# Two decode attentions in one kernel: wq as nine rows per partition, both sides' q from one set of matmuls

## The chip, the cores and the metric

The kernel runs on one core of one Trainium2 chip. The metric is the device time of one execution in microseconds. The core has five engines with an instruction stream each: TensorE (PE, with its weight loads listed apart as PEld), VectorE (DVE), ScalarE (ACT), GpSimd (POOL) and SyncE (SP). 16 DMA engines move data between HBM and the on-chip memory of 128 partitions (SBUF). TensorE writes into PSUM, eight banks of 128 x 512 float32.

## The reference

Two independent decode steps, A and B, each for one token; their outputs are put side by side. Everything is bfloat16.

```python
Hq, Dh = 32, 128          # 16 kv heads, Sk = 8192, x is [1, 1, 576]
q = (x @ wq).reshape(B, Sq, Hq, Dh).transpose(0, 2, 1, 3)      # wq is [576, 4096]
k = jnp.repeat(k_cache[:, :, Sk - W:, :], rep, axis=1)         # A: the last W = 2048 keys; B: all 8192
v = jnp.repeat(v_cache[:, :, Sk - W:, :], rep, axis=1)
p = softmax(einsum("bhqd,bhkd->bhqk", q, k) * (Dh ** -0.5))
o = einsum("bhqk,bhkd->bhqd", p, v)
out = o.transpose(0, 2, 1, 3).reshape(B, Sq, Hq * Dh) @ wo     # wo is [4096, 576]
```

All inputs together are 102.76 MB: the two wq and the two wo have 4.72 MB each, A's keys and values 8.39 MB each, B's 33.55 MB each.

## The kernel before

**How it is written.** The kernel is a list of operations for each engine (`Prog`, L37). An operation names the operations and loads that it waits for, and `emit` (L59) turns the names into semaphore waits. The order on an engine is the order in which the operations were written down; an engine that waits holds up everything behind it on that engine.

**The loads.** All big loads are issued by SP, in one order, onto one DMA queue. They go into a ring in SBUF of 144 KB per partition (`ring`, `RING` L31). `place` (L167) gives each load the next stretch of the ring; where the stretch was used before, SP waits ahead of the issue for the last users of what lay there. Each load has one of 24 semaphores in turn; from the 25th load on SP also waits for the users of the load 24 places earlier. The order is: wq of A (two loads), wq of B (two loads), K of A's first four heads (K0), K1, V0, K2, V1, K3, V2, the K of B's first four heads in two halves (K4.0, K4.1), V3, K5 in two halves, V4, K6, V5, K7, V6, V7 in two halves, then wo of A in one load and wo of B in five. (A unit is four kv heads: units 0 to 3 are A's, 4 to 7 are B's.) The first eight loads have free room in the ring. V1 and K3 take the place of the main load of A's wq, V2 that of A's last rows and of the start of B's wq, K4.0 that of the rest of B's wq and of K0.

**wq.** wq of a side has 576 rows of 8 KB. The main load brings the first 512 rows: partition p holds rows 4p to 4p + 3, 32 KB (L191). The second load, "tail", brings the last 64 rows as 128 half rows of 4 KB: partition p holds half p mod 2 of row 512 + p // 2 (L193). A's and B's wq lie one after the other in the ring and both use all 128 partitions.

**x.** ACT's queue loads the two x into one partition (`xrow`). For each side (L266), DVE copies the last 64 elements of x twice each (`xd`, L267); five matmuls of depth 1 against a row of ones put x on the partitions and repeat it over 128 columns (`xT`, L276); DVE casts the four main columns to bf16 (`xr`, L279), and multiplies the fifth by `par`, 1 on even or on odd partitions, for the left and the right half rows (L282).

**The q matmuls.** For each side and each of eight column blocks of 512 (L299 to L313), five matmuls of depth 128 add up a block of q in one of four PSUM banks; since x is repeated over the columns of the stationary operand, all 128 output rows are the same q. 80 matmuls in all; the first 40 need only A's wq, the last 40 only B's. ACT copies each block into `qsb` (`qe`, L314), DVE turns two blocks at a time in 32 x 32 squares into `ktb` (`qT`, L317), and after a side's last turn four DVE copies put the pieces into the stationary operands of the score matmuls, `za` for A (`z0`, L329) and `zb` for B (`z1`, L324).

**The rest.** Then unit after unit: DVE turns K slabs of 2048 elements per partition out of the ring into `ktb` (`turn`, L350; the first one waits for all eight `z` copies, since `ktb` held q), PE makes scores (`score`, L367), DVE and PE find the maximum, ACT takes the exponential (L406), DVE turns the probabilities (L414, L418), and PE multiplies with V out of the ring (`pv`, L431). At the end PE multiplies the outputs with wo (`F`, L510), first A's, then B's as its five loads land, and two output transfers follow (L523).

Of the kernel before, what the change touches and what calls it, by code (L numbers as in the profile page):

```python
# [14 lines left out]
DM = 576  # L15
# [4 lines left out]
SLAB = 2048  # L20
NQ = G // 4
# [4 lines left out]
W0 = 2 * (NB - 1)  # L26
ZW = 128 + W0
ZA = 128 + 24
BIG = 1e30
N0 = 320  # L30
RING = 72 * 1024  # L31
NSEM = 24
NKT = 3
NWO = [[32], [17, 8, 4, 2, 1]]


class Prog:  # L37
# [60 lines left out]
def bass_concat_heads__sliding_block_cached__gqa_block_cached__decode_kernel(nc, A_x, A_k_cache, A_v_cache, A_wq, A_wo,  # L98
                         B_x, B_k_cache, B_v_cache, B_wq, B_wo, out):
    xs, ks, vs = [A_x, B_x], [A_k_cache, B_k_cache], [A_v_cache, B_v_cache]  # L100
    wqs, wos = [A_wq, B_wq], [A_wo, B_wo]
# [4 lines left out]
    ring = nc.alloc_sbuf_tensor("ring", [128, RING], BF16)  # L106
    ktb = nc.alloc_sbuf_tensor("ktb", [128, NKT * SLAB], BF16)
# [3 lines left out]
    onesf = nc.alloc_sbuf_tensor("onesf", [128, 128], F32)  # L111
    onesb = nc.alloc_sbuf_tensor("onesb", [1, 128], BF16)
    xrow = nc.alloc_sbuf_tensor("xrow", [1, 2 * DM], BF16)
    xdup = nc.alloc_sbuf_tensor("xdup", [1, 2, 128], BF16)
    xrep = nc.alloc_sbuf_tensor("xrep", [128, 2, 6, 128], BF16)
    qsb = nc.alloc_sbuf_tensor("qsb", [128, 4, 512], BF16)

    zb = nc.alloc_sbuf_tensor("zb", [128, NQ, 4, ZW], BF16)

    za = nc.alloc_sbuf_tensor("za", [128, NQ, 4, ZA], BF16)  # L120
# [17 lines left out]
    par = nc.alloc_sbuf_tensor("par", [128, 2], F32)  # L138
# [9 lines left out]
    sb = [nc.alloc_psum_tensor("sb%d" % b, [128, 512], F32) for b in range(2)]  # L148
    qb = [nc.alloc_psum_tensor("qb%d" % b, [128, 512], F32) for b in range(2)]
    vb = [nc.alloc_psum_tensor("vb%d" % b, [128, 512], F32) for b in range(2)]  # L150
    mb = nc.alloc_psum_tensor("mb", [128, 512], F32)
    ob = nc.alloc_psum_tensor("ob", [128, 512], F32)

    def view(t, free, offset, dims, parts=128, p0=0):
        return bass.AP(tensor=t, offset=p0 * free + offset, ap=[[free, parts], *dims])

    pg = Prog(nc)
    op, load = pg.op, pg.load
    s_x = [nc.alloc_semaphore("s_x%d" % i) for i in range(2)]
    s_ld = [nc.alloc_semaphore("s_ld%d" % i) for i in range(NSEM)]  # L160
    s_out = nc.alloc_semaphore("s_out")
    s_row = [nc.alloc_semaphore("s_row%d" % i) for i in range(2)]

# [3 lines left out]
    def place(size, uses, issue, name):  # L167
        if at[0] + size > RING:
            at[0] = 0
        lo, hi = at[0], at[0] + size  # L170
        at[0] = hi
        deps = []
        for r in list(live):
            if r[0] < hi and lo < r[1]:
                deps += r[2]
                live.remove(r)
        n = nload[0]
        nload[0] += 1
        if n >= NSEM:
            deps += uses_of[n - NSEM]  # L180
        uses_of.append(list(uses))
        live.append((lo, hi, list(uses)))
        t = ring[:, lo:hi]
        load("sp", lambda e: issue(e, t), s_ld[n % NSEM], 16 * (n // NSEM + 1), deps=deps, name=name)
        return t

    wq_at = {}
    w = HQ * DH
    for P in range(2):
        uses = ["qmm%d.7" % P]  # L190
        main = wqs[P][0:512, :].rearrange("(p k) n -> p (k n)", k=4)  # L191
        wq_at[P, 0] = place(4 * w, uses, lambda e, t, main=main: e.dma_start(t, main), "wq%d.0" % P)
        tail = wqs[P][512:DM, :].rearrange("r (c n) -> (r c) n", c=2)  # L193
        wq_at[P, 1] = place(w // 2, uses, lambda e, t, tail=tail: e.dma_start(t, tail), "wq%d.1" % P)


    kv_at = {}
# [35 lines left out]
    def slab(kind, i, s):  # L233
# [10 lines left out]
       deps=["id0"], name="ident")  # L244
# [6 lines left out]
    for P in range(2):  # L251
        x = xs[P]
# [7 lines left out]
    for c in range(2):  # L260
        op("dve", lambda e, c=c: e.tensor_reduce(par[:, c:c + 1], view(identf, 128, c, [[2, 64]]), AX.X, ALU.add),
           deps=["identf"], name="par%d" % c)


    banks = [sb[0], sb[1], qb[0], qb[1]]
    for P in range(2):  # L266
        op("dve", lambda e, P=P: e.tensor_copy(  # L267
            view(xdup, 256, 128 * P, [[2, 64], [1, 2]], parts=1),
            view(xrow, 2 * DM, P * DM + 512, [[1, 64], [0, 2]], parts=1)), deps=["x%d" % P], name="xd%d" % P)
        for k in range(5):  # L270
            def mm(e, P=P, k=k):
                if k < 4:
                    lhsT = view(xrow, 2 * DM, P * DM + k, [[4, 128]], parts=1)
                else:
                    lhsT = xdup[0:1, P, :]
                return e.matmul(banks[2 * P + k // 4][:, (k % 4) * 128:(k % 4 + 1) * 128], lhsT=lhsT,  # L276
                                rhs=onesb[0:1, :], start=True, stop=True)
            op("pe", mm, deps=["x%d" % P, "onesb", "xd%d" % P], name="xT%d.%d" % (P, k))
        op("dve", lambda e, P=P: e.tensor_copy(  # L279
            xrep[:, P, 0:4, :].rearrange("p k m -> p (k m)"), banks[2 * P][:, :]), deps=["xT%d.3" % P], name="xr%d.0" % P)  # L280
        for c in range(2):
            op("dve", lambda e, P=P, c=c: e.tensor_scalar(  # L282
                xrep[:, P, 4 + c, :], banks[2 * P + 1][:, 0:128], par[:, c:c + 1], None, ALU.mult),
                deps=["xT%d.4" % P, "par%d" % c], name="xr%d.%d" % (P, 1 + c))

    op("dve", lambda e: e.tensor_reduce(clsb[:].rearrange("p (b r) -> p b r", r=2),
                                        view(identf, 128, 0, [[32, 4], [1, 2], [2, 16]]), AX.X, ALU.add),
       deps=["identf"], name="clsb")
    op("dve", lambda e: e.tensor_reduce(clsa[:], view(identf, 128, 0, [[1, 8], [8, 16]]), AX.X, ALU.add),
       deps=["identf"], name="clsa")  # L290
# [2 lines left out]
    op("dve", lambda e: e.tensor_scalar(mkl[:], view(ident, 128, 0, [[0, 16], [1, 4], [0, 2]], 4), -1.0, BIG,  # L293
                                        ALU.add, ALU.mult), deps=["ident"], name="mkl")

    XR = ["xr%d.%d" % (P, c) for P in range(2) for c in range(3)]

    KT = NKT * SLAB
    for P in range(2):  # L299
        for n in range(8):  # L300
            u = 8 * P + n
            bank = banks[u % 4]

            def mm(e, P=P, n=n, bank=bank):
                for k in range(5):
                    if k < 4:
                        lhsT, o = xrep[:, P, k, :], wq_at[P, 0][:, k * w + n * 512:k * w + (n + 1) * 512]
                    else:
                        lhsT, o = xrep[:, P, 4 + n // 4, :], wq_at[P, 1][:, (n % 4) * 512:(n % 4 + 1) * 512]
                    ins = e.matmul(bank[:, :], lhsT=lhsT, rhs=o, start=(k == 0), stop=(k == 4))  # L310
                return ins
            op("pe", mm, deps=["wq%d.0" % P, "wq%d.1" % P] + XR + (["qe%d" % (u - 4)] if u >= 4 else []),
               name="qmm%d.%d" % (P, n))  # L313
            op("act", lambda e, u=u, bank=bank: e.activation(qsb[:, u % 4, :], bank[:, :], ACT.Copy),  # L314
               deps=["qmm%d.%d" % (P, n)] + (["qT%d" % (u // 2 - 2)] if u >= 4 else []), name="qe%d" % u)
            if n % 2:
                op("dve", lambda e, u=u, n=n: e.transpose(  # L317
                    ktb[:, (n - 1) * 512:(n + 1) * 512].bitcast(I32),
                    qsb[:, u % 4 - 1:u % 4 + 1, :].rearrange("p a n -> p (a n)").bitcast(I32)),
                    deps=["qe%d" % (u - 1), "qe%d" % u] + (["z0.%d" % i for i in range(4)] if P else []),  # L320
                    name="qT%d" % (u // 2))
        for b in range(4):
            if P == 1:
                op("dve", lambda e, b=b: e.tensor_copy(  # L324
                    view(zb, NQ * 4 * ZW, 32 * b + W0, [[4 * ZW, NQ], [2 * ZW, 2], [ZW, 2], [1, 2]], 32, 32 * b),
                    view(ktb, KT, b * 256, [[1024, NQ], [64, 2], [1, 2], [128, 2]], 32, 32 * b)),
                    deps=["qT%d" % u for u in range(4, 8)] + ["zb0"], name="z1.%d" % b)
            else:
                op("dve", lambda e, b=b: e.tensor_copy(  # L329
                    view(za, NQ * 4 * ZA, ZA - 128 + 32 * b, [[4 * ZA, NQ], [2 * ZA, 2], [ZA, 2], [1, 8]], 32, 32 * b),  # L330
                    view(ktb, KT, 0, [[1024, NQ], [64, 2], [1, 2], [128, 8]], 32, 32 * b)),
                    deps=["qT%d" % u for u in range(4)] + ["za0"], name="z0.%d" % b)
    Z = ["%s.%d" % (z, b) for z in ("z0", "z1") for b in range(4)]
    QE = ["qe%d" % u for u in range(16)]


    k0 = [sum(nslab[:i]) for i in range(NU)]
# [218 lines left out]
```

## Time and profile before

| | before |
|---|---|
| three runs | 246.38, 246.15, 246.25 us (median 246.25) |
| span of the profiled execution | 245.2 us; its own run time is not given apart |
| DMA queue 1 (all big loads) | 4468 packets, 102.76 MB, 97.9% of 16 engines' span |
| PE, DVE, ACT, POOL busy | 172.3, 129.1, 24.3, 8.2 us |
| TensorE clock granted, mean | 0.82 of full speed |
| q matmuls (L310) | first at 14.60 us, last ends at 34.6 us |
| first K turn (L350) | 36.86 us |
| wo of A landed, PE starts on it | 232.3 us |

Stages are read from the windows: busy time of each engine between two moments, then the granted clock, the DMA engines' busy share and GB/s. A packet is counted into a window by its start, so a share can exceed 1. The trace also keeps every DMA packet with its start, duration and size, but not the engine that moved it; a load over 128 partitions is 128 packets, eight per engine, and one 4-byte packet per engine that marks the end of its share. The matmul record is nearly complete (79 of 80 of the q matmuls are in it).

### The profile page before, as it was taken

To read this page: it belongs to the slowest core of one execution; us is meant where nothing else is said; L and a number is where in the kernel's file an instruction comes from. 1 tells how busy PE (TensorE), PEld (TensorE's weight loads), DVE (VectorE), ACT (ScalarE), POOL (GpSimd) and SP (SyncE) were. 2 spreads that over 40 slices of the span, in tenths; PEclk is the share of its full clock that TensorE was granted. 3 is DMA by queue.
4 is the path that set the end of the run, shared out by engine and by line. 5 is a ranking of instruction groups with operands and counts; after the bars stand their busy time and mean duration, and the time that the engine had idled before them with its cause. 6 is when DMAs were issued, how large, how long until landed. Compare 5 with 4: busy or idle time off the path is not lost.

```text
span 245.2 us, 2253 instructions
## 1 busy us (share of the span) xinstructions
PE 172.3 (70%) x960; PEld 71.8 (29%) x961; DVE 129.1 (53%) x162; ACT 24.3 (10%) x52; POOL 8.2 (3%) x15
## 2 busy tenths in 40 slices
PE   0269967787867994889582869945579939257197
PEld 0124422224433222432130523211423213213154
DVE  0422547667789986699501699810679920500201
ACT  2004540021201000100000100000010000200001
POOL 8400000000000000000000000000000000000000
PEclk9999995789999997569957578989657985677559
DMA  7999999999999999998999999999999999999994
GB/s 267 420 457 410 437 428 425 433 428 457 440 430 387 468 428 428 452 470 385 406 428 425 438 476 428 438 406 425 438 466 460 395 406 430 428 438 409 430 407 158
DMA packets 4481, 102.90 MB, mean 420 GB/s; under 512 B 500, under 2 KB 632, under 8 KB 1144
## 3 DMA queue, kind: packets, MB, share of 16 engines
q1 hardware_dynamic: 4468, 102.76, 97.9%
q8 instruction: 7, 0.11, 0.2%
q14 instruction: 2, 0.02, 0.0%
q10 hardware_dynamic: 4, 0.00, 0.0%
HBM read 102.76 MB, written 0.00 MB: 419 GB/s over the span
## 4 chain that ended last, share of the span: by engine, by line
DMA 55%; PE 29%; DVE 12%; ACT 2%; issue 2%; SPq 0%; DVEq 0%
DMA ring<-in_B_v_cache_dram 40%; DMA ring<-in_A_wo_dram 10%; DVE ktb L350 9%; PE vb L431 8%; DMA ring<-in_A_wq_dram 5%; PE qb L367 5%; PE qb L510 5%; PE sb L310 5%; PE qb L310 4%; ACT psb L406 1%; DVE pta L414 1%; PE ob L447 1%; PE sb L367 1%; PE qb L359 1%; PE mb L397 1%
## 5 line engine op out<-in xcount | busy, mean ns | idle before, releaser
L350 DVE STREAM_TRANSPOSE ktb<-ring 128x1024 int32<-128x1024 int32 x80 | 92.8, 1211 | 29.5 <-DMA ring<-in_B_k_cache_dram 28.3
L367 PE MATMUL sb<-ktb,zb 128*128 128x512 bf16 x256 | 76.0, 437 | 23.7 <-DVE ktb L350 21.1
L367 PEld LDWEIGHTS sb<-ktb,zb 128*128 128x128 bf16 x256 | 23.4, 106 | 72.4 <-DVE ktb L350 45.9
L431 PE MATMUL vb<-ring,pts 128*32 128x512 bf16 x256 | 24.7, 567 | 18.5 <-DMA ring<-in_B_v_cache_dram 14.4
L367 PE MATMUL qb<-ktb,za 128*128 128x512 bf16 x64 | 19.4, 449 | 2.8 <-DVE ktb L350 2.8
L431 PEld LDWEIGHTS vb<-ring,pts 128*32 128x32 bf16 x256 | 9.0, 134 | 33.6 <-DMA ring<-in_B_v_cache_dram 16.7
L438 ACT ACTIVATE xo<-vb 128x512 f32<-128x512 f32 x8 | 4.8, 597 | 129.4 <-PE vb L431 129.4
L418 DVE STREAM_TRANSPOSE pts<-psb 32x512 bf16<-32x512 bf16 x16 | 11.3, 703 | 9.5 <-ACT psb L406 9.3
L510 PE MATMUL qb<-ring,oP 128*1 128x256 bf16 (+1 forms) x128 | 11.3, 340 | 4.0 <-DMA ring<-in_A_wo_dram 4.0
L317 DVE STREAM_TRANSPOSE ktb<-qsb 128x512 int32<-128x512 int32 x8 | 5.7, 711 | 15.0 <-ACT qsb L314 15.0
L310 PE MATMUL sb<-ring,xrep 128*128 128x512 bf16 x40 | 11.4, 442 | 2.7 <-DMA ring<-in_A_wq_dram 2.7
L447 PEld LDWEIGHTS ob<-sel,xo 128*128 128x128 f32 x64 | 10.9, 244 | 3.8 <-ACT xo L438 2.2
L447 PE MATMUL ob<-sel,xo 128*128 128x8 f32 x64 | 10.1, 285 | 1.2 <-ACT xo L438 1.2
L367 PEld LDWEIGHTS qb<-ktb,za 128*128 128x128 bf16 x64 | 6.1, 109 | 13.4 <-issue 5.8
L310 PE MATMUL qb<-ring,xrep 128*128 128x512 bf16 x39 | 9.5, 393 | 0.0
L510 PEld LDWEIGHTS qb<-ring,oP 128*1 128x1 bf16 x128 | 7.0, 93 | 8.3 <-DMA ring<-in_A_wo_dram 4.1
L521 DVE CAST outsb<-qb 1x256 bf16<-1x256 f32 x2 | 0.8, 420 | 14.7 <-PE qb L510 14.7
L491 DVE RECIPROCAL rl<-mb 128x64 f32<-128x64 f32 x1 | 0.6, 558 | 12.3 <-PE mb L488 12.3
L276 PE MATMUL sb<-onesb,xrow 1*128 1x128 bf16 x4 | 0.6, 298 | 9.2 <-DVE xdup L267 9.2
L392 DVE TENSOR_REDUCE mr<-mb 1x8 f32<-1x128 f32 x8 | 1.9, 240 | 9.5 <-PE mb L384 9.5
L310 PEld LDWEIGHTS sb<-ring,xrep 128*128 128x128 bf16 x40 | 4.3, 109 | 8.6 <-issue 5.3
L314 ACT ACTIVATE qsb<-sb 128x512 bf16<-128x512 f32 x8 | 4.8, 597 | 19.1 <-PE sb L310 19.1
(65 smaller groups left out, 68.8 us busy)
## 6 DMA issues: line engine op xcount, KB each, us to landing
ring<-in_B_k_cache_dram SPq DMA_DIRECT2D x8, 4096.0 KB, 24.5
ring<-in_A_k_cache_dram SPq DMA_DIRECT2D x4, 2048.0 KB, 30.5
ring<-in_A_v_cache_dram SPq DMA_DIRECT2D x4, 2048.0 KB, 25.4
ring<-in_B_v_cache_dram SPq DMA_DIRECT2D x2, 4096.0 KB, 23.8
ring<-in_A_wo_dram SPq DMA_DIRECT2D x1, 4608.0 KB, 23.9
ring<-in_A_wq_dram SPq DMA_DIRECT2D x1, 4096.0 KB, 12.5
ring<-in_B_wq_dram SPq DMA_DIRECT2D x1, 4096.0 KB, 22.6
ring<-in_B_wo_dram SPq DMA_DIRECT2D x1, 2448.0 KB, 29.3
```

Source lines behind the costliest of these rows:

```text
L310: ins = e.matmul(bank[:, :], lhsT=lhsT, rhs=o, start=(k == 0), stop=(k == 4))
L314: op("act", lambda e, u=u, bank=bank: e.activation(qsb[:, u % 4, :], bank[:, :], ACT.Copy), deps=["qmm%d.%d" % (P, n)] + (["qT%d" % (u // ...
L317: op("dve", lambda e, u=u, n=n: e.transpose(ktb[:, (n - 1) * 512:(n + 1) * 512].bitcast(I32), qsb[:, u % 4 - 1:u % 4 + 1, :].rearrange("p ...
L350: op("dve", lambda e: e.transpose(kt.bitcast(I32), src.bitcast(I32)), deps=[landed] + (["S%d" % (k - NKT)] if k >= NKT else Z), name="T%d. ...
L359: e.matmul(bank[:, :], lhsT=mkl[:].rearrange("p a h r -> p (a h r)"), rhs=mkr[:].rearrange("p q h -> p (q h)"), start=True, stop=False)
L367: ins = e.matmul(bank[:, :], lhsT=lhsT, rhs=view(ktb, KT, (k % NKT) * SLAB + 64 * c + v, [[128, 16], [2, 32]]), start=(side == "B" and s = ...
L397: op("pe", lambda e: e.matmul(mb[:, 128:129], lhsT=mexp[0:1, :], rhs=onesf[0:1, 0:1], start=True, stop=True), deps=["mx%d" % i, "ones"], n ...
L418: op("dve", lambda e, b=b: e.transpose(view(pts, NB * 128, 2 * b, [[8, 16], [128, NB], [1, 2]], 32, 32 * b), psb[32 * b:32 * b + 32, :]), ...
L431: ins = e.matmul(vbank[i][32 * j:32 * j + 32, :], lhsT=lhsT, rhs=src[:, 512 * j:512 * j + 512], start=(s == 0), stop=(s == nslab[i] - 1))
L438: op("act", lambda e: e.activation(xo[:, c, :], vbank[i][:, :], ACT.Copy), deps=["V%d.%d" % (i, nslab[i] - 1)] + (["O%d" % (i - 1)] if i e ...
L447: ins = e.matmul(ob[:, at:at + 8], lhsT=xo[:, c, 128 * t:128 * t + 128], rhs=sel[:, 8 * t:8 * t + 8], start=(t == 0), stop=(t == 3))
L510: ins = e.matmul(fb[r:r + 1, 0:hi - lo], lhsT=oP[:, P, k0 + k:k0 + k + 1], rhs=wo_at[P, c][:, k * DM + lo:k * DM + hi], start=(k0 + k == 0 ...
```

## The change

wq of both sides becomes one matrix of 1152 rows in nine rows per partition: partition 2j holds rows 9j to 9j + 8 of A's wq (72 KB), partition 2j + 1 the same rows of B's. It is loaded in two steps, rows 0 to 3 of each partition (32 KB) and rows 4 to 8 (40 KB), and each step has one load for A, over the 64 even partitions, and one for B, over the 64 odd ones: four loads as before, and the same stretch of the ring. Only A's loads go through `place`; B's use two semaphores of their own (`s_wq`).

x is laid out to match: A's and B's elements are interleaved in groups of nine in `xint` (two DVE copies), nine matmuls of depth 1 put them on the partitions, and six DVE operations multiply with `par` while casting, so that the left 64 columns of the stationary operand hold A's x on even partitions and zero elsewhere, and the right 64 columns B's x on odd partitions. One matmul then gives A's q in output rows 0 to 63 and B's in rows 64 to 127. There are 9 x 8 = 72 matmuls: first four rows times eight blocks, each block in its own PSUM bank, which need the first step of both sides; then for each block the other five rows, which need the second step. A block is complete only at the end, after which come eight evictions, four turns, and all eight `z` copies after the last turn.

```diff
+KW = DM // 64
+KW0 = 4
-    xdup = nc.alloc_sbuf_tensor("xdup", [1, 2, 128], BF16)
-    xrep = nc.alloc_sbuf_tensor("xrep", [128, 2, 6, 128], BF16)
-    qsb = nc.alloc_sbuf_tensor("qsb", [128, 4, 512], BF16)
+    xint = nc.alloc_sbuf_tensor("xint", [1, 2 * DM], BF16)
+    xrep = nc.alloc_sbuf_tensor("xrep", [128, KW, 128], BF16)
+    qsb = nc.alloc_sbuf_tensor("qsb", [128, 8, 512], BF16)
...
-    for P in range(2):
-        uses = ["qmm%d.7" % P]
-        main = wqs[P][0:512, :].rearrange("(p k) n -> p (k n)", k=4)
-        wq_at[P, 0] = place(4 * w, uses, lambda e, t, main=main: e.dma_start(t, main), "wq%d.0" % P)
-        tail = wqs[P][512:DM, :].rearrange("r (c n) -> (r c) n", c=2)
-        wq_at[P, 1] = place(w // 2, uses, lambda e, t, tail=tail: e.dma_start(t, tail), "wq%d.1" % P)
+    def load_wq(e, P, lo, k0, k1):
+        src = wqs[P].rearrange("(p k) n -> p (k n)", k=KW)[:, k0 * w:k1 * w]
+        return e.dma_start(bass.AP(tensor=ring, offset=P * RING + lo, ap=[[2 * RING, 64], [1, (k1 - k0) * w]]), src)
+
+    wq_at = []
+    for c, (k0, k1) in enumerate(((0, KW0), (KW0, KW))):
+        lo = k0 * w
+        t = place((k1 - k0) * w, ["qmm%d" % (3 if c == 0 else 11)],
+                  lambda e, t, lo=lo, k0=k0, k1=k1: load_wq(e, 0, lo, k0, k1), "wq%d.0" % c)
+        load("sp", lambda e, lo=lo, k0=k0, k1=k1: load_wq(e, 1, lo, k0, k1), s_wq[c], 16, name="wq%d.1" % c)
+        wq_at += [t[:, k * w:(k + 1) * w] for k in range(k1 - k0)]
...
-            op("pe", mm, deps=["x%d" % P, "onesb", "xd%d" % P], name="xT%d.%d" % (P, k))
-        op("dve", lambda e, P=P: e.tensor_copy(
-            xrep[:, P, 0:4, :].rearrange("p k m -> p (k m)"), banks[2 * P][:, :]), deps=["xT%d.3" % P], name="xr%d.0" % P)
...
+    banks = [*sb, *qb, *vb, mb, ob]
+    for P in range(2):
+        op("dve", lambda e, P=P: e.tensor_copy(
+            view(xint, 2 * DM, KW * P, [[2 * KW, 64], [1, KW]], parts=1),
+            view(xrow, 2 * DM, P * DM, [[KW, 64], [1, KW]], parts=1)), deps=["x%d" % P], name="xi%d" % P)
+    for k in range(KW):
+        op("pe", lambda e, k=k: e.matmul(
+            banks[k // 4][:, (k % 4) * 128:(k % 4 + 1) * 128], lhsT=view(xint, 2 * DM, k, [[KW, 128]], parts=1),
+            rhs=onesb[0:1, :], start=True, stop=True), deps=["xi0", "xi1", "onesb"], name="xT%d" % k)
+    XR = []
+    for k0 in range(0, KW, 4):
+        n = min(4, KW - k0)
+        for P in range(2):
+            XR.append("xr%d.%d" % (k0, P))
+            op("dve", lambda e, k0=k0, n=n, P=P: e.tensor_scalar(
+                xrep[:, k0:k0 + n, 64 * P:64 * P + 64], view(banks[k0 // 4], 512, 64 * P, [[128, n], [1, 64]]),
+                par[:, P:P + 1], None, ALU.mult), deps=["xT%d" % (k0 + n - 1), "par%d" % P], name=XR[-1])
...
+    def qmm(e, n, k):
+        return e.matmul(banks[n][:, :], lhsT=xrep[:, k, :], rhs=wq_at[k][:, n * 512:(n + 1) * 512],
+                        start=(k == 0), stop=(k == KW - 1))
+
+    for k in range(KW0):
+        def mm(e, k=k):
+            for n in range(8):
+                ins = qmm(e, n, k)
+            return ins
+        op("pe", mm, deps=["wq0.0", "wq0.1"] + XR, name="qmm%d" % k)
+    for n in range(8):
+        def mm(e, n=n):
+            for k in range(KW0, KW):
+                ins = qmm(e, n, k)
+            return ins
+        op("pe", mm, deps=["wq1.0", "wq1.1"], name="qmm%d" % (KW0 + n))
+        op("act", lambda e, n=n: e.activation(qsb[:, n, :], banks[n][:, :], ACT.Copy),
+           deps=["qmm%d" % (KW0 + n)], name="qe%d" % n)
+        if n % 2:
+            op("dve", lambda e, n=n: e.transpose(
+                ktb[:, (n - 1) * 512:(n + 1) * 512].bitcast(I32),
+                qsb[:, n - 1:n + 1, :].rearrange("p a n -> p (a n)").bitcast(I32)),
+                deps=["qe%d" % (n - 1), "qe%d" % n], name="qT%d" % (n // 2))
+    QT = ["qT%d" % i for i in range(4)]
+    for b in range(4):
+        op("dve", lambda e, b=b: e.tensor_copy(
+            view(za, NQ * 4 * ZA, ZA - 128 + 32 * b, [[4 * ZA, NQ], [2 * ZA, 2], [ZA, 2], [1, 8]], 32, 32 * b),
+            view(ktb, KT, 0, [[1024, NQ], [64, 2], [1, 2], [128, 8]], 32, 32 * (b % 2))),
+            deps=QT + ["za0"], name="z0.%d" % b)
+    for b in range(4):
+        op("dve", lambda e, b=b: e.tensor_copy(
+            view(zb, NQ * 4 * ZW, 32 * b + W0, [[4 * ZW, NQ], [2 * ZW, 2], [ZW, 2], [1, 2]], 32, 32 * b),
+            view(ktb, KT, b * 256, [[1024, NQ], [64, 2], [1, 2], [128, 2]], 32, 64 + 32 * (b % 2))),
+            deps=QT + ["zb0"], name="z1.%d" % b)
```

More of the change, by code (lines that the diff above doesn't have):

```diff
@@ L160, in bass_concat_heads__sliding_block_cached__gqa_block_cached__decode_kernel @@
     s_ld = [nc.alloc_semaphore("s_ld%d" % i) for i in range(NSEM)]
+    s_wq = [nc.alloc_semaphore("s_wq%d" % i) for i in range(2)]
     s_out = nc.alloc_semaphore("s_out")
@@ L185, in place @@
         return t
-    wq_at = {}
     w = HQ * DH
-    for P in range(2):
-        uses = ["qmm%d.7" % P]
-        main = wqs[P][0:512, :].rearrange("(p k) n -> p (k n)", k=4)
-        wq_at[P, 0] = place(4 * w, uses, lambda e, t, main=main: e.dma_start(t, main), "wq%d.0" % P)
-        tail = wqs[P][512:DM, :].rearrange("r (c n) -> (r c) n", c=2)
-        wq_at[P, 1] = place(w // 2, uses, lambda e, t, tail=tail: e.dma_start(t, tail), "wq%d.1" % P)
+    def load_wq(e, P, lo, k0, k1):
[8 more added lines that the diff above has]
+        wq_at += [t[:, k * w:(k + 1) * w] for k in range(k1 - k0)]
     kv_at = {}
@@ L262, in bass_concat_heads__sliding_block_cached__gqa_block_cached__decode_kernel @@
            deps=["identf"], name="par%d" % c)
-    banks = [sb[0], sb[1], qb[0], qb[1]]
+    banks = [*sb, *qb, *vb, mb, ob]
     for P in range(2):
         op("dve", lambda e, P=P: e.tensor_copy(
[L268 to L277, printed above, removed]
-            op("pe", mm, deps=["x%d" % P, "onesb", "xd%d" % P], name="xT%d.%d" % (P, k))
-        op("dve", lambda e, P=P: e.tensor_copy(
-            xrep[:, P, 0:4, :].rearrange("p k m -> p (k m)"), banks[2 * P][:, :]), deps=["xT%d.3" % P], name="xr%d.0" % P)
[L281 to L284, printed above, removed]
+            view(xint, 2 * DM, KW * P, [[2 * KW, 64], [1, KW]], parts=1),
[12 more added lines that the diff above has]
+                par[:, P:P + 1], None, ALU.mult), deps=["xT%d" % (k0 + n - 1), "par%d" % P], name=XR[-1])
     op("dve", lambda e: e.tensor_reduce(clsb[:].rearrange("p (b r) -> p b r", r=2),
@@ L294, in bass_concat_heads__sliding_block_cached__gqa_block_cached__decode_kernel @@
                                         ALU.add, ALU.mult), deps=["ident"], name="mkl")
-    XR = ["xr%d.%d" % (P, c) for P in range(2) for c in range(3)]
     KT = NKT * SLAB
[L299 to L332, printed above, removed]
@@ L333, in bass_concat_heads__sliding_block_cached__gqa_block_cached__decode_kernel @@
     Z = ["%s.%d" % (z, b) for z in ("z0", "z1") for b in range(4)]
-    QE = ["qe%d" % u for u in range(16)]
+    QE = ["qe%d" % n for n in range(8)]
     k0 = [sum(nslab[:i]) for i in range(NU)]
```

## The prediction

> **What bounds the kernel now.** First the page's top, its 40 slices and its queues.
>
> ```profile
> span 245.2 us, 2253 instructions
> PE 172.3 (70%) x960; PEld 71.8 (29%) x961; DVE 129.1 (53%) x162; ACT 24.3 (10%) x52; POOL 8.2 (3%) x15
> DMA  7999999999999999998999999999999999999994
> q1 hardware_dynamic: 4468, 102.76, 97.9%
> q8 instruction: 7, 0.11, 0.2%
> ```
>
> No compute engine is above 70%, while the 16 DMA engines are full in nearly every slice; queue 1 alone fills 97.9% of the span. The windows say it by stage; the row's last two columns are the DMA engines' busy share and GB/s.
>
> ```profile
> 0.00:1.70 1.70, 0.00 (x0) 0.00 (x0) 0.00 (x0) 0.97 (x1) 0.92 (x9) 1.00 0.00 0
> ...
> 12.00:24.00 12.00, 9.40 (x32) 3.82 (x33) 3.37 (x9) 3.18 (x6) 0.00 (x0) 1.00 0.98 421
> 24.00:100.00 76.00, 60.59 (x301) 25.42 (x301) 54.27 (x68) 12.60 (x28) 0.00 (x0) 0.90 1.01 431
> 100.00:200.00 100.00, 73.24 (x340) 27.34 (x338) 62.95 (x64) 4.01 (x11) 0.00 (x0) 0.77 1.01 433
> ```
>
> So the time is 1.8 us before the first packet, 241.1 us of packets, and about 2.4 us from the last landing (242.9, by the trace's packets) to the end. Is a transfer ever issued too late? The chain of waits seems to say that compute matters up to 92.8 us:
>
> ```profile
> 14.60 4.43 PE sb L310 x10
> ...
> 36.86 1.26 DVE ktb L350
> ...
> 92.75 0.02 issue
> 92.77 0.02 SPq L83
> 92.79 0.03 issue
> 92.82 30.94 DMA ring<-in_B_v_cache_dram
> ```
>
> But that load, 128 x 64 KB = 8.39 MB, needs only 19.4 us at the 433 GB/s of the window; of its 30.94 us it queued some 11. I laid the trace's packets against SP's issues: this load's first packet starts at 102.21, 9.39 us after its issue, and that is the smallest such distance of all loads behind wq (next: 10.16 for A's wo, 10.95, 10.99). **Compute may come 9.4 us later anywhere before 92.8 us without one idle DMA cycle.**
>
> Packets by size (from the same record, medians): 4 KB 0.159 us, 16 KB 0.614, 32 KB 1.213 to 1.215, 36 KB 1.368, 64 KB 2.422.
>
> **The change, part by part.**
>
> *The loads.* Same bytes, same four issues on SP. Per DMA engine, wq was 16 packets of 32 KB and 16 of 4 KB; it becomes 8 of 32 KB and 8 of 40 KB. No row shows 40 KB; between 1.368 (36 KB) and 2.422 (64 KB), at 36 KB's rate, it is 1.520. So 8 x 1.213 + 8 x 1.520 = 21.86 replaces 16 x 1.213 + 16 x 0.159 = 21.95: **-0.09 us**, on the path. What no row shows is a load over every second partition; all loads of before take 128. Its bounds: from the same 1.213 per 32 KB packet to twice that, if two DMA engines had to share one way into the memory (rival 1). I take 1.213, because no row here depends on the partition: sizes from 16 to 64 KB run at 26.7 to 27.1 GB/s an engine.
>
> The Trainium skill speaks against the change here: "SBUF — State Buffer", section "Door 1: The DMA port swizzle", says that bandwidth follows how many of 16 ports the partitions reach and that partitions 0 to 63 get half. By its formula, though, the lowest two bits of a partition's number do not enter, so every second partition reaches all 16 ports, and the sum by it stays at -0.09. "DMA: Bandwidth & Descriptors", section "The descriptor swizzle", gives each DMA engine one port for a 128-partition load and does not say what 64 rows two apart do; no trace here shows it.
>
> *SP's queue.* Nothing is added ahead of K0. Two placed loads fewer shift which semaphore each later load uses; the loads from the 25th on wait for users of the first ones, over for 150 us. The second V load waits for the first 32 q matmuls instead of qmm0.7 (25.96); the third for the last q matmul, as before (34.59). Their first packets start at 43.99 and 53.77: 18 and 19 us of room.
>
> *x.* Out: two copies of 128 elements (1.01 and 0.20), 10 small matmuls, two casts of 0.69, four scalings of 0.34. In: two copies of 576 elements, 9 matmuls, six masked scalings (256 elements: between the 0.34 of 128 and the 0.69 of 512, say 0.45; the last pair 0.3). A copy costs between 0.9 and 4.5 (4.5 times each old one); I take 0.9, as the 1.01 holds the start after a wait. B's x landed just before 10.5: 10.5 + 0.9 + 9 matmuls 1.3 + scalings 2.0 = 14.7, at worst 18.3. Before, the matmuls began at 14.57 on the wq wait. The new first half (8 packets of 32 KB an engine, as the old A main load) is in at 12.9, so the first q matmul waits for DVE, not the DMA. New wait; behind it on PE stand only the q matmuls.
>
> *The q matmuls.* 80 become 72. Cold they took 0.443 (14.60, 4.43 for 10), warm 0.216 (2.16 for 10). First half: 32, of them 10 cold: 4.4 + 4.8 = 9.2, to 23.9. Second half's data: 24.2 to 25.1 as before; PE starts at about 25.5, 40 x 0.216 = 8.6, to 34.1. After the last: eviction 0.61, turn 0.72, then all eight placing copies (1.24 + 0.79; before only 0.79 stood here): first K turn at 37.5 against 36.86. If the short idle makes PE cold throughout, 40 x 0.443 = 17.7 and the turn comes at 46.6, **9.7 us** late: about the room. Eight evictions (0.597) and four turns (0.711) fewer save engine time that nobody waits for: worth 0, covered by the DMA queue; without cover the warm case costs 0.6.
>
> *Sum.* 245.2 - 0.09 = 245.1 of span. The three runs' median 246.25 lies 1.0 above the span (the profiled run's own time is not given); so **246.15 us**.
>
> **What sets the end inside the DMA.** Each load ends on each engine with a 4-byte mark. On the first load the 16 marks run from 12.07 to 12.56, and one more comes at 12.88: its engine's first packet took 2.37 where the others took 1.75 to 2.15. The gap of 0.33 stays until the last load. Also, the seven 16 KB code loads (queue 8) each set one engine back by about 1.55; one hits that same engine at 132. The last engine's lag is the end.
>
> **Rivals.**
> 1. *Shared ways, slower.* If the generator hands 64 rows out in plain fours, two engines write through the same way at once. Place: wq's 16 packets per engine; price: 21.86 more, **268.0 us**. It decides once those packets average over 1.022 times their time (0.49 of 21.9). For: no row shows such a load. Against: loads are dealt so evenly now that marks lie within 0.8 us.
> 2. *The late engine, faster.* The first packets are other reads. If none is 0.3 later than the rest and the lag engine no longer ends last: -0.33; four packets per DMA and engine instead of eight may also start the later engines sooner: first packets start over 1.76 to 2.05, at most -0.15. With -0.09: -0.57, **245.7**. Against: 0.33 is one engine's one packet, and another with a code load then stands 0.4 behind it.
> 3. *Another engine hit, slower.* Eight matmuls with their weight loads and one small matmul fewer move every code load; if one hits the lagging engine twice, +1.55: **247.7**. Against: in this profile seven loads hit seven engines.
> 4. *Compute eats the room, slower.* Cold second half and a slow x (18.3): the first K turn 13.3 late, 3.9 beyond the 9.4: **250.1**. Against: the PE clock stands at 1.0 from 14 to 36 us, with gaps of 2.7 us.
> 5. *The change does not do what it says:* if the two half loads do not meet in one matmul, wq is read as now and the time stays: inside the forecast.
>
> **How the numbers follow.** Forecast (with 5) 0.70, rival 2 0.13, rival 1 0.07, rival 3 0.06, rival 4 0.04. A measurement of this kernel tells about 0.2% (0.49 us) from no change. Rival 2 is the case of faster (0.13), 1, 3 and 4 of slower (0.17), the forecast's own range, 245.8 to 246.6 (the first packets' spread either way, 0.3 to 0.4), is the same (0.70). The 80% range reaches down to rival 2's 245.6 and a little towards rival 3, to 246.8; what is left out is rivals 1 and 4, most of 3 and the ends, 0.18.
>
> **What would show it.** Right: queue 1 as full as now; the windows behind 24 us at 1.01; wq in by 25.1; first K turn at 37 to 38; V4 issued 8 to 10 us ahead of its first packet; last landing near 242.8. Wrong: 32 KB packets of wq far over 1.22 us (rival 1); a slice with idle DMA near 100 us (rival 4); marks of the last load spread over more than 2.5 us (rival 3) or under 2.1 (rival 2).

## The result, and the profile after

The changed kernel takes **246.86 us** (median of 16 runs, 246.67 to 247.15) against 246.31 us of the kernel before (16 runs, 246.15 to 246.51): ratio **1.0022, 95% interval 1.0016 to 1.0029**. It is 0.55 us slower. The forecast was 246.15 with a range of 245.6 to 246.8; the time lies 0.06 outside, on the side to which the forecast had given 0.17.

The first view of the profile after is the page's top, its engines, its slices and its queues:

```profile
span 245.2 us, 2215 instructions
PE 168.5 (69%) x952; PEld 70.3 (29%) x952; DVE 126.2 (51%) x158; ACT 19.5 (8%) x44; POOL 8.1 (3%) x15
...
DMA  7999999999999999998999999989999899999994
...
q1 hardware_dynamic: 4212, 102.76, 97.8%
...
q14 instruction: 1, 0.01, 0.0%
```

Queue 1 is as full as before with 256 packets fewer, and the windows behind 24 us are still saturated:

```profile
24.00:100.00 76.00, 60.06 (x299) 24.45 (x300) 53.15 (x67) 11.91 (x27) 0.00 (x0) 0.91 1.00 427
100.00:200.00 100.00, 68.97 (x334) 26.04 (x332) 62.58 (x64) 3.09 (x8) 0.00 (x0) 0.81 1.01 435
```

So the DMA engines still bound the kernel, and the loss has to lie before their first packet, in their packets, or outside all of it. Two readings find it.

**The span hardly moved.** For every run both the time and the span are recorded. Mean over the runs:

| | runs | time minus span | span |
|---|---|---|---|
| before (all comparisons with experiments) | 101 | 1.32 us | 245.03 us |
| changed | 16 | 1.68 us | 245.19 us |

Of the 0.55 us, **0.35 us lie outside the span** and 0.16 inside (the remaining 0.04 comes of using means, and these 101 runs of before in place of the 16 beside the changed kernel, whose spans are not on record). The profiled execution of before had a span of 245.2, at the upper end of its runs; that hid the part inside the span in the two pages, and no page shows the part outside.

**The first load starts later.** SP's issues, before and then after (start, duration, what):

```profile
0.73 0.41 SPq L192 DMA_DIRECT2D ring<-in_A_wq_dram  x1
1.20 0.41 SPq L194 DMA_DIRECT2D ring<-in_A_wq_dram  x1
```

```profile
0.73 0.56 SPq L194 DMA_DIRECT2D ring<-in_A_wq_dram  x1
1.34 0.58 SPq L194 DMA_DIRECT2D ring<-in_B_wq_dram  x1
```

The issue takes 0.56 instead of 0.41, and by the trace's packets the first one starts at 2.07 instead of 1.76: 1.34 after the start of the issue instead of 1.03. So about half of the 0.31 is the longer issue; the other half comes behind its end (0.78 us to the first packet instead of 0.62). The first packets of the 16 DMA engines start on average at 2.30 instead of 1.91.

Compute, off the path, by the timeline of after (start, duration, line, what, idle before and its end):

```profile
25.61 4.00 PE L304 MATMUL sb<-ring,xrep 128*128 128x512 bf16 x10 [2.36 <-DMA ring<-in_B_wq_dram]
...
34.84 1.24 PE L304 MATMUL ob<-ring,xrep 128*128 128x512 bf16 x5
...
36.75 0.71 DVE L322 STREAM_TRANSPOSE ktb<-qsb 128x512 int32<-128x512 int32 x1 [1.45 <-ACT qsb L319]
37.50 1.23 DVE L328 COPY za<-ktb 32x128 bf16<-32x128 bf16 x4
38.76 0.79 DVE L333 COPY zb<-ktb 32x32 bf16<-32x32 bf16 x4
39.66 3.50 DVE L354 STREAM_TRANSPOSE ktb<-ring 128x1024 int32<-128x1024 int32 x3
```

The first K turn comes at 39.66, 2.8 us later than before, and V4, B's first V load, is issued at 95.57, 6.93 us ahead of its first packet (before 9.39). That is still room: by the trace's packets none of the 16 DMA engines is without one between 6 and 240 us, in either kernel.

### The profile page after: what moved, and what is told of

It is laid out like the page before. It is cut to its first block, busy times and chain, and to the rows that moved or that the text cites. A ratio compares the mean times of both kernels' runs of the same rounds, so it can differ in the third digit from the quotient of the medians.

```text
span 245.2 us, 2215 instructions
## 1 busy us (share of the span) xinstructions
PE 168.5 (69%) x952; PEld 70.3 (29%) x952; DVE 126.2 (51%) x158; ACT 19.5 (8%) x44; POOL 8.1 (3%) x15
## 3 DMA queue, kind: packets, MB, share of 16 engines
q1 hardware_dynamic: 4212, 102.76, 97.8%
## 4 chain that ended last, share of the span: by engine, by line
DMA 61%; PE 21%; DVE 12%; ACT 2%; issue 2%; SPq 1%; DVEq 0%
DMA ring<-in_B_v_cache_dram 39%; DMA ring<-in_B_wo_dram 13%; DVE ktb L354 9%; DMA ring<-in_B_wq_dram 9%; PE vb L435 7%; PE qb L371 5%; PE sb L304 2%; ACT psb L410 1%; DVE pta L418 1%; PE ob L451 1%; PE vb L304 1%; PE qb L304 1%; PE sb L371 1%; SPq L237 1%; PE qb L363 1%
## 5 line engine op out<-in xcount | busy, mean ns | idle before, releaser
L371 PE MATMUL sb<-ktb,zb 128*128 128x512 bf16 x256 | 73.1, 424 | 23.3 <-DVE ktb L354 20.6
L371 PEld LDWEIGHTS sb<-ktb,zb 128*128 128x128 bf16 x256 | 22.8, 104 | 70.1 <-DVE ktb L354 45.7
L435 PE MATMUL vb<-ring,pts 128*32 128x512 bf16 x256 | 23.6, 546 | 21.1 <-DMA ring<-in_B_v_cache_dram 17.1
L435 PEld LDWEIGHTS vb<-ring,pts 128*32 128x32 bf16 x256 | 8.5, 130 | 35.4 <-DMA ring<-in_B_v_cache_dram 19.2
L322 DVE STREAM_TRANSPOSE ktb<-qsb 128x512 int32<-128x512 int32 x4 | 2.8, 711 | 21.3 <-ACT qsb L319 21.3
L304 PE MATMUL sb<-ring,xrep 128*128 128x512 bf16 x18 | 7.3, 546 | 4.9 <-DMA ring<-in_B_wq_dram 4.9
L279 PE MATMUL sb<-onesb,xint 1*128 1x128 bf16 x8 | 1.1, 307 | 9.7 <-DVE xint L275 9.7
L363 PE MATMUL qb<-mkr,mkl 4*128 4x512 bf16 x4 | 1.8, 439 | 7.2 <-DVE ktb L354 7.2
L386 DVE TENSOR_REDUCE mx<-qb 128x1 f32<-128x512 f32 x4 | 2.8, 691 | 6.3 <-PE qb L371 6.3
L304 PE MATMUL qb<-ring,xrep 128*128 128x512 bf16 x18 | 5.6, 436 | 0.0
```

The source lines that it names most:

```text
L304: return e.matmul(banks[n][:, :], lhsT=xrep[:, k, :], rhs=wq_at[k][:, n * 512:(n + 1) * 512], start=(k == 0), stop=(k == KW - 1))
L322: op("dve", lambda e, n=n: e.transpose(ktb[:, (n - 1) * 512:(n + 1) * 512].bitcast(I32), qsb[:, n - 1:n + 1, :].rearrange("p a n -> p (a n ...
L363: e.matmul(bank[:, :], lhsT=mkl[:].rearrange("p a h r -> p (a h r)"), rhs=mkr[:].rearrange("p q h -> p (q h)"), start=True, stop=False)
L371: ins = e.matmul(bank[:, :], lhsT=lhsT, rhs=view(ktb, KT, (k % NKT) * SLAB + 64 * c + v, [[128, 16], [2, 32]]), start=(side == "B" and s = ...
L386: op("dve", lambda e: e.tensor_reduce(mx[:, 0:1], sbank[i][:, :], AX.X, ALU.max), deps=["S%d" % (k0[i] + nslab[i] - 1)] + (["mT%d" % (i - ...
L435: ins = e.matmul(vbank[i][32 * j:32 * j + 32, :], lhsT=lhsT, rhs=src[:, 512 * j:512 * j + 512], start=(s == 0), stop=(s == nslab[i] - 1))
```

## The experiments

All ratios are to the kernel before, run beside it on the same chip, with their 95% intervals. "First packet" is the start of the earliest packet of the first load, from the span's start; a span is the mean over the runs where nothing else is said.

### What in the first load is late: source, destination, or compute

`e1_src_contig`: the changed kernel, each load from one contiguous stretch.

```diff
-        src = wqs[P].rearrange("(p k) n -> p (k n)", k=KW)[:, k0 * w:k1 * w]
+        src = wqs[P][64 * k0:64 * k1, :].rearrange("(p k) n -> p (k n)", k=k1 - k0)
...
```

> The changed kernel, but each of the four wq loads reads one contiguous stretch of HBM (partition j of a side holds rows 4j to 4j+3 in the first step and rows 256+5j to 260+5j in the second, instead of rows 9j to 9j+8); x is laid out to match with four copies instead of two. Destinations and sizes are those of the change. Late-start theory (the first load's first packet starts 1.48 us after its issue instead of 1.03, and the packets after it are as fast as before): if the source's pitch of 72 KB is what makes the first packets late, the first packet comes at 1.8 to 1.9 and the time falls to 246.2 to 246.4, ratio to before 0.999 to 1.0005. If the 64 destination rows on every second partition make it late, the first packet stays at 2.2 and the ratio at 1.002 (246.8). Rival, the loads are not the cause but the new order of compute is: ratio stays at 1.002 with a first packet at 1.8.

(The right figures of the changed kernel are 1.34 and 2.07, not the 1.48 and the 2.2 in it.) Measured: 247.06 us, ratio 1.0028 (1.0018 to 1.0038), first packet at 2.09, span 245.41. The source's pitch is not the cause of the late start. The span is even 0.22 longer than the changed kernel's; in the profiled runs each engine's first packet takes 2.11 us on average here, 1.89 there.

`e2_before_pitch`: the kernel before with a pitch alone, 36 KB from row to row (the change has 72).

```diff
-        main = wqs[P][0:512, :].rearrange("(p k) n -> p (k n)", k=4)
+        main = bass.AP(tensor=wqs[P].tensor, offset=wqs[P].offset, ap=[[9 * w // 2, 128], [1, 4 * w]])
```

> The kernel before, but the main wq load of each side reads 128 rows of 32 KB at a pitch of 36 KB instead of one contiguous 4 MB; everything else is the same (the rows are not the right ones, so the output is not the reference's). Late-start theory with the source's pitch as its cause: first packet at 2.1 to 2.2 instead of 1.76, time +0.3 to +0.5, ratio 1.0012 to 1.002. With the destination as cause: first packet at 1.76, ratio 1.000.

Measured: 246.37 us, ratio 0.9999 (0.9990 to 1.0008), first packet at 1.76. The same answer from the other side, though at half the change's pitch.

`e3_loads128`: the change's compute on 128-partition loads, three of them instead of four.

```diff
...
+    t0 = place(4 * w, ["qmm3"], lambda e, t: e.dma_start(t, main), "wq0.0")
+    t1 = place(5 * w, ["qmm11"], lambda e, t: e.dma_start(t[:, 0:9 * w // 2], whole), "wq1.0")
...
+    load("sp", lambda e: e.dma_start(t1[:, 9 * w // 2:5 * w], tail), s_wq[1], 16, name="wq1.1")
...
```

> The changed kernel's compute with 128-partition loads under it: wq of A in 128 rows of 32 KB (4 MB) for the first step, wq of B in 128 rows of 36 KB and A's last 64 rows as 128 pieces of 4 KB for the second; all three contiguous in HBM, same bytes and same places in the ring, same 72 matmuls (the data do not fit the matmuls, so the output is not the reference's). Late-start theory: first packet at 1.76 as before and ratio 0.999 to 1.0005, though compute is that of the change. Rival, compute or code of the changed kernel is the cause: ratio 1.002 as for the change.

Measured: 246.57 us, ratio 1.0008 (0.9999 to 1.0017), first packet at 1.75. Inside the span it is 0.30 faster than the changed kernel (244.89 against 245.19), whose compute it shares: its first packet comes 0.32 sooner. It is also 0.18 faster than before (245.07). That is not the change's own gain, since the loads are neither the change's nor those of before: by the packets' medians they take 21.89 us on an engine, those of before 21.95, so most of the 0.18 is unexplained. Time minus span is 1.70. So the 0.35 outside the span come with the change's compute, and the late start with its loads; each theory had half of it.

`e4_before_late`: the price of a late start by itself.

```diff
+        if n == 0:
+            deps = deps + ["id0"]
         load("sp", lambda e: issue(e, t), s_ld[n % NSEM], 16 * (n // NSEM + 1), deps=deps, name=name)
```

> The kernel before, but SP waits ahead of its first issue for GpSimd's clearing of ident, which ends at 1.07 us; so all first loads are issued 0.35 to 0.4 us later and nothing else changes. Late-start theory: the time before the first packet is on the path one for one, time +0.35 to +0.4, ratio 1.0014 to 1.0016. Rival, the start is hidden behind something later (a wait in the last stage, or the slowest engine's lag): ratio 1.000.

Measured: 246.79 us, ratio 1.0015 (1.0006 to 1.0024). The first issue moved from 0.73 to 1.09, the first packet from 1.76 to 2.13, and the mean span by 0.41: within the scatter of the spans, one for one. The start is on the path in full.

### The partitions themselves

`e7_halves`: A on the lower, B on the upper 64 partitions.

```diff
-        ... bass.AP(tensor=ring, offset=P * RING + lo, ap=[[2 * RING, 64], [1, (k1 - k0) * w]]), src)
+        ... bass.AP(tensor=ring, offset=64 * P * RING + lo, ap=[[RING, 64], [1, (k1 - k0) * w]]), src)
```

> The changed kernel with A's wq on partitions 0 to 63 and B's on 64 to 127 instead of even and odd ones; x keeps its masks for even and odd, so the q of both sides are mixed and the output is not the reference's. Same sizes, sources and queue. Shared-way theory (the prediction's rival 1, and the Trainium skill's SBUF page, section Door 1): 64 partitions in one half are reached at half the rate, wq's 32 KB packets take about 2.4 us, wq is in at 46 to 47 instead of 25, the ratio is 1.085 to 1.09. If partitions do not matter to the rate: packets of 1.21 and a ratio of 1.002. First packet: if 64 rows are what makes the start late, 1.34 us after the issue as in the changed kernel (2.07 from the span's start); if the step of two does, 1.03 (1.76).

Measured: 270.07 us, ratio 1.0965 (1.0951 to 1.0980), somewhat more than expected. A 32 KB packet takes 2.56 us (median), a 40 KB one 3.20, and wq is in at 48.1 instead of 25.1. The windows (engines, clock, DMA share, GB/s in the last columns):

```profile
0.00:24.00 24.00, 1.37 (x10) 1.05 (x11) 4.01 (x14) 1.49 (x2) 8.15 (x15) 1.00 0.96 202
24.00:48.00 24.00, 8.70 (x32) 3.36 (x30) 0.00 (x0) 0.00 (x0) 0.00 (x0) 0.79 0.97 201
48.00:100.00 52.00, 39.92 (x189) 15.97 (x190) 30.79 (x45) 9.42 (x20) 0.00 (x0) 0.84 1.01 429
```

The DMA engines are as busy as ever and move half: busy is not fast. So what the prediction's rival 1 feared does happen to a 64-row load, and costs 23.2 us over the changed kernel; laying the two sides on even and odd partitions avoids it. That the engines share a way here was not seen, only their doubled packets. The Trainium skill's "SBUF — State Buffer", section "Door 1: The DMA port swizzle", says that partitions 0 to 63 reach only 8 of the 16 ports. This case's 201 to 202 GB/s, against 429 behind wq, agree with it.

The first packet starts at 2.08 here too. So the late start does not come from the step of two; what all late wq loads have in common is their 64 rows.

### Half a microsecond minus the start: what lies outside the span

`e5_before_sem4` and `e6_after_sem22`: the change adds two semaphores; here their number is raised in the one and lowered in the other kernel.

```diff
 # e5, on the kernel before
+    s_idle = [nc.alloc_semaphore("s_idle%d" % i) for i in range(4)]
 # e6, on the changed kernel
-NSEM = 24
+NSEM = 22
```

> The kernel before with four more semaphores that nothing uses. In the runs so far the time is 1.34 us longer than the span with the kernel before and its variants (37 semaphores), and 1.67 to 1.7 longer with the changed kernel and its variants (39). Semaphore theory: about 0.165 us outside the span for each semaphore of the program, so time minus span becomes 2.0, the span stays at 245.05 and the time rises by 0.66, ratio 1.0027. Rival, the length of the engines' programs or the way x and q are computed makes the 0.33: ratio 1.000.

> The changed kernel with 22 ring semaphores instead of 24, so 37 in all as before; the order of loads and waits on the queue is the same. Semaphore theory: time minus span falls from 1.67 to 1.34, time 246.5, ratio to before 1.0008 (the rest is the late start: span 245.2 against 245.05). Rival (program length, compute): ratio stays 1.0022.

Measured: 246.28 us, ratio 0.9999 (0.9991 to 1.0008), time minus span 1.31; and 246.83 us, ratio 1.0021 (1.0013 to 1.0030), time minus span 1.70. The semaphore theory fell in both.

What the two groups of kernels do differ in is a code load, a transfer of queue 14, which the page lists as "instruction". The page of before has this line, in which the packets of 8 KB lie at 66.1 and 182.3 us; the changed kernel (its line is above) has only one, at 68.8:

```profile
q14 instruction: 2, 0.02, 0.0%
```

In all 14 profiled runs it is so: the kernels at about 1.32 have the late one, those at about 1.68 lack it.

`e9_act_pad` and `e10_dve_pad`: programs made as long as before, one engine each (`pad` is a scratch tensor).

```diff
 # e9
...
+    for i in range(14):
+        op("act", lambda e, i=i: e.activation(pad[:, 4 * i:4 * i + 4], warm[:, 0:4], ACT.Exp))
 # e10
...
+    for i in range(8):
+        op("dve", lambda e, i=i: e.tensor_copy(pad[:, i:i + 1], par[:, 0:1]), deps=["par0"])
```

> The changed kernel with 14 tiny ACT activations at 2.7 to 6 us, where ACT is idle, so that ACT's program has as many instructions as before (the change took eight evictions and six waits out of it). In every run so far the kernels whose time is 1.33 us over the span have a code load of 8 KB on queue 14 near 182 us, and those at 1.67 do not; ACT has few instructions left by 182 us, so it could be ACT's. Program-end theory: an engine that has not fetched the last piece of its program during the run fetches it after the span. If that engine is ACT: the load near 182 us (or earlier) is back, time minus span is 1.33, time 246.5, ratio 1.0009. If not: 1.67 and ratio 1.0022.

> The changed kernel with eight tiny DVE copies at 2.3 to 3 us, where DVE is idle, so that DVE's program is no shorter than before (the change took six instructions out of it). Program-end theory with DVE as the engine: a second 8 KB code load on queue 14 late in the run is back and time minus span is 1.33, ratio 1.0009. If the engine is ACT, as I expect: 1.67 and ratio 1.0022, within 0.0005 of the changed kernel. Rival for both: no code load matters and the 0.33 stays in both runs.

Measured: with 14 more ACT instructions 246.46 us, ratio 1.0006 (0.9997 to 1.0015), time minus span 1.33, and the load is back at 182.5 us. With eight more DVE instructions 246.80 us, ratio 1.0018 (1.0009 to 1.0027), time minus span 1.67, one 8 KB load, at 68.7. Queue 14 in the pages of `e9` and `e10`:

```profile
q14 instruction: 3, 0.02, 0.0%
```

```profile
q14 instruction: 1, 0.01, 0.0%
```

(The third packet in `e9` is one of 96 bytes at 0.12 us.) The traces hold 69 instructions of ACT, its waits and issues counted, before, 55 after the change and 69 again in `e9`. **With the fourteen ACT instructions fewer, eight evictions and six waits, the change loses 0.34 us outside the span**; fourteen useless instructions at a moment when ACT is idle give it back. That ACT then fetches the last piece of its program after the span is the theory that found this; the runs show the effect and the missing load, not the fetch.

### The start: can it be had back

`e8_k0_first`: a 128-partition load in front.

```diff
+    pg.ops["sp"].insert(0, pg.ops["sp"].pop(4))
```

> The changed kernel with K0 (128 partitions) issued ahead of the four wq loads, same places in the ring. Late-start theory: the first packets are K0's; if they start at 1.76 as those of the old wq load, the span is 245.05 - 0.09 = 244.9 and the ratio 1.001 with the 0.33 outside the span left. wq lands 4.9 us later, so the fourth B V load keeps about 2 us of its 6.9 us of room and nothing else changes. If K0's own first packet is as late as wq's (its source has one more dimension, its issue takes 0.62): ratio 1.002.

Measured: median 246.82 us, ratio 1.0034 (1.0017 to 1.0050), twelve runs from 246.43 to 248.48, spans from 244.8 to 246.8. K0's first packet is as late as wq's (2.14; its issue takes 0.63), yet the best five spans, 244.8 to 244.9, are 0.3 to 0.4 under the changed kernel's mean. In the profiled run (span 246.3) the loads from K1 up to V4 (B's first V load; the expectation calls it the fourth) are 0.3 to 0.4 ahead of the changed kernel's. The chain of waits shows V4's issue:

```profile
100.53 0.02 SPq L85
100.57 23.64 DMA ring<-in_B_v_cache_dram
```

Its first packet starts at 102.12, 1.55 after the issue, where the start alone takes 1.02 to 1.41 on an empty queue. The room is used up: from 102.57 to 103.21 up to three of the 16 DMA engines have no packet, which happens nowhere else between 9 and 240 us. The next load starts 0.3 us *behind* the changed kernel's, later ones up to 0.6, and the last landing is 1.1 behind. So the lead is lost where the room ends; what adds the rest up to 1.1, and why other runs kept the lead, was not settled.

The gain of the runs with the best spans had to come from something other than an earlier start: K0's first packets, of 16 KB, took 0.77 us on average, 0.16 over the usual 0.614, while wq's first packets of 32 KB take 1.89 in the changed kernel, 0.67 over 1.213.

`e11_first_8k` and `e12_before_first_8k`: A's first wq load cut into one row of 8 KB per partition and the other three, in the changed kernel and in the one before (there with a semaphore `s_first` of its own; the q matmuls wait for the new load too).

```diff
 # e11
-                  lambda e, t, lo=lo, k0=k0, k1=k1: load_wq(e, 0, lo, k0, k1), "wq%d.0" % c)
+                  lambda e, t, lo=lo, k0=k0, k1=k1: load_wq(e, 0, lo, k0, k1 if k0 else 1), "wq%d.0" % c)
+        if c == 0:
+            load("sp", lambda e: load_wq(e, 0, w, 1, KW0), s_wq[2], 16, name="wq0.2")
...
 # e12
+        n = 1 if P == 0 else 4
+        wq_at[P, 0] = t0 = place(4 * w, uses, lambda e, t, main=main, n=n: e.dma_start(t[:, 0:n * w], main[:, 0:n * w]),
...
```

> The changed kernel with its first wq load cut in two: A's first row per partition (64 packets of 8 KB) and then A's other three rows (64 of 24 KB). With K0 first (16 KB packets) the first 16 packets took 0.16 us more than later ones of that size, with wq first (32 KB) 0.67 more, and the undisturbed runs were 0.35 us faster in the span though the packets began no sooner. First-read theory: the extra of the first packets goes with their size, so 8 KB first packets lose 0.1 to 0.15 each instead of 0.67, span 244.7 and ratio 1.0000 to 1.0006 (the 0.33 outside the span is left). Rival, the gain with K0 first came from something else: span 245.2, ratio 1.0022 or more, as one load more is issued.

> The kernel before with A's main wq load cut in two: the first row per partition (128 packets of 8 KB), then the other three rows (128 of 24 KB). First-read theory: the first 16 packets lose 0.3 instead of 0.7 (as with 8 KB first in the changed kernel), so the span falls from 245.05 to 244.7 to 244.85, time minus span stays 1.33, ratio 0.9985 to 0.9993; it would beat both kernels by little. Rival: one load more costs what the smaller first packets save: ratio 1.000.

Measured in the changed kernel: 246.68 us, ratio 1.0013 (1.0004 to 1.0021), mean span 244.99 instead of 245.19, first packets 0.62 on average, 0.31 over the usual 0.307. They lose 0.36 less than the changed kernel's and the span gains 0.20, less than half of the 0.5 that was expected; where the rest went was not settled. In the kernel before: **245.95 us, ratio 0.9986 (0.9977 to 0.9995)**, mean span 244.65, time minus span 1.32; the first packets took 0.68, 0.37 over the usual, instead of 1.96, 0.75 over. It beats both kernels. The page's lines:

```profile
span 244.6 us, 2255 instructions
...
q1 hardware_dynamic: 4612, 102.76, 98.1%
```

One more load and 144 records more in queue 1 than before, and still faster: the span gains 0.36, and the first packets lose 0.38 less. Size alone does not set what a first packet loses, though: K0's 16 KB packets lost less (0.16) than these of 8 KB.

## Why the prediction was wrong, point by point

- **What bounds the kernel** held. Queue 1 at 97.8%, the windows at 1.00 and 1.01; compute was delayed by 2.8 us and no load noticed. Of the signs named for "right", wq was in by 25.06 and the last landing came at 242.80, as forecast; the first K turn and V4's 6.93 us lay outside theirs, off the path. None of the signs could see the larger part of the loss, which lies outside the span.
- **The loads' packets** held: 40 KB took 1.514 (forecast 1.520), 32 KB 1.213, which makes 21.82 on an engine and a gain of 0.13 instead of 0.09. No run shows this gain by itself.
- **"What no row shows is a load over every second partition ... I take 1.213"** was right for the rate and asked too little. The form was priced per packet; its start was taken over from the 128-partition row (1.03 from issue to first packet), and rival 2 even allowed a gain of 0.15 there. It takes 1.34: **+0.31 for the earliest packet, +0.39 on the mean** of the two profiled runs. The +0.31 less the packets' 0.09 to 0.13 leaves about 0.2, near the +0.16 seen in the span. (The variants agree: 244.99 and 245.05 in `e5` and `e2`, with the old start, 245.13 to 245.19 in `e6`, `e9` and `e10`, with the new one.) This is the first term of the sum that failed: one left out, not one mis-sized. The start stood in the prediction as "1.8 us before the first packet", a constant; `e4_before_late` shows that it is on the path one for one.
- **"The three runs' median 246.25 lies 1.0 above the span"** failed, and it carried the larger part. One profiled span was set against the median of other runs, and the difference was held to be the same for both kernels. It is 1.32 before and 1.68 after. That 1.0 was read for 1.32 cancels in the sum; that it was held constant does not. "Eight evictions (0.597) and four turns (0.711) fewer save engine time that nobody waits for: worth 0" is where the cause stood: the evictions' time is worth nothing, but their absence, with that of six waits, cost 0.34 (`e9_act_pad`).
- **SP's queue** held: V1 issued at 23.28 and V2 at 36.12, 18 to 21 us ahead of their packets.
- **x** came out better than costed: B's x was in at 8.92 (before 10.12), the two copies take 1.65 together and the six scalings 2.1, so the first q matmul waits for wq, at 13.40, not for DVE (forecast 14.7). Off the path.
- **The q matmuls**: the second half did not stay warm. PE idled for 2.36 us, and the window 25.60 to 29.60 has a granted clock of 0.57 where those around it have 1.00; the first ten matmuls took 4.00. The first K turn came at 39.66 instead of 37.5. The price named for the all-cold case, 9.7, was an upper end; about a quarter came, inside the room. The remark against rival 4, a clock of 1.0 from 14 to 36 us with gaps of 2.7, misread the trace: its record of the clock begins at 19.8 us, and the ten matmuls behind that gap took 0.443 each, twice the later ones' 0.216.
- **Rivals.** 1: the slowdown is real (`e7_halves`), and the layout avoids it. 2: wrong in sign for the start, but its remark that the first packets are the odd ones led to `e12`; the late engine it builds on is no trait of the kernel (in `e5`, with the same loads, the last two of the 16 marks come at 12.65 and 12.80, and the last landing at 242.63). 3 did not occur: as far as the packets' times tell the engines apart, each of the seven 16 KB code loads again set another one back. 4: not in the change; `e8_k0_first` shows the room giving out. 5 did not occur: queue 1 has 256 packets fewer. None of the five contained what happened, two small costs that add up: the 0.17 given to "slower" stood on other causes.

## What to carry to other kernels

When a kernel is bound by its DMA queue, the time from launch to the first packet and the first packet itself are path: look at the form of the very first load (rows, size per row) separately from the rate of the rest, and try smaller packets there (here 8 KB instead of 32 KB won 0.36 us). Compare time minus span between the two kernels before explaining a sub-microsecond difference by the trace; here an engine's shorter program cost 0.34 us there. And lay two 64-row loads on even and odd partitions rather than on halves, which cost 23.2 us here.

## What the runs showed of the hardware that was not expected

- From the start of SP's issue to the first packet: 1.02 to 1.04 us for 128 rows with a two-dimensional pattern (six kernels), 1.34 to 1.37 for 64 rows (seven kernels, with contiguous or pitched source, with a partition step of one or two), 1.41 for 128 rows with a source of one dimension more. The issue itself takes 0.41, 0.56 to 0.58 and 0.63 of it; 0.62 to 0.63, 0.77 to 0.81 and 0.78 come behind its end. What in the form costs it is open.
- The first packet of each DMA engine takes longer than the later ones: on average 0.54 to 0.90 us more at 32 KB (ten kernels; 0.75 before, 0.67 after), 0.31 and 0.37 at 8 KB, 0.16 at 16 KB (K0). In `e7_halves` it does not: 2.24 against 2.56.
- 64 partitions in one half of the memory take a wq packet to 2.1 times its duration (2.56 for 1.213, 3.20 for 1.514), while the DMA engines show as 0.96 and 0.97 busy; 64 on every second partition cost nothing per packet (1.213, as with 128 partitions).
- An ACT program shorter by 14 instructions cost 0.34 us outside the span, with one 8 KB code load fewer in the span.
- After PE stood idle for 2.36 us in the changed kernel, the granted clock was 0.57 over the next 4 us.
